# A new order of tasks for a pre-norm block of Infini attention and a dense MLP, on one core

## The chip, the core and the metric

The kernel runs on one core of a Trainium2 chip. A core has a matrix engine (TensorE, PE in the profile), a vector engine (VectorE, DVE), an activation engine (ScalarE, ACT), a general engine (GpSimd, POOL), and a queue from which this kernel issues all its transfers (SyncE, SP). They run side by side and wait for one another on semaphores. The metric is the device time of one execution in microseconds (us); smaller is better.

## The reference

A sequence of 2048 tokens with 640 features goes through one transformer block:

```python
h  = x + attention(layernorm(x))
h2 = h + silu(layernorm(h) @ w1) @ w2          # w1: 640 x 1728, w2: 1728 x 640
```

The attention has 32 heads of 20 features and goes through the sequence in 4 segments of 512 tokens. Each segment does causal softmax attention inside itself, and reads a memory that holds the segments before it:

```python
for s in range(4):
    p     = softmax(q_s @ k_s.T * scale + mask);  a_dot = p @ v_s
    pq    = phi(q_s)                               # phi(t) = t + 1 if t > 0 else exp(t)
    a_mem = (pq @ M) / (pq @ z + 1e-6)
    o_s   = g * a_mem + (1 - g) * a_dot            # g = sigmoid(beta), per head
    M += phi(k_s).T @ v_s;  z += phi(k_s).sum()
out = concat(o_s) @ wo
```

Inputs and output are in bf16.

## The kernel before

The kernel is a list of 1313 tasks with declared reads and writes. `build` declares them segment by segment, and `Graph.schedule` (L291 on) walks through the list `ORDER`, in which the tasks' numbers stand, and gives each its buffer slot and a planned start. What the program keeps of this is the order on each engine, the buffers, and the number of filler matmuls on a zero tile in the first microseconds. Each engine works strictly through its own list; `Tracker` puts in the semaphore waits that the data ask for. The string `ENGINE` says for each task which engine does it (p, a, d, g, s for PE, ACT, DVE, POOL, SP), and `BANK` which PSUM bank a result gets. So an instruction that waits holds up all that follow on its engine, and a transfer that cannot be issued yet holds up all transfers behind it.

The planned times come from costs in the source: for compute tasks a duration, for transfers a time on SP, a time `bw` on the shared transfer engines, and a time until landing. They are never seen by the chip.

The names of the tasks, with segment `s`, token block `b` (of 128 tokens) or chunk `c` (of four heads and some):

- `x{b}`, `w_k0`, `w_q0`, `w_wv`, `w_wo*`: loads of tokens and weights. `w_w1_0` to `w_w1_4` and `w_w2_0` to `w_w2_8` are the MLP's weights.
- `re_wq{j}`, `re_wk{j}`: pieces of the q and k weights copied into a layout with 32 columns a head (`wqr`, `wkr`, L798 and L799), on ScalarE, VectorE or GpSimd.
- `n1_st`, `n1_rs`, `n1_ap`, `n1_tr` (and `n2_...` before the MLP): statistics, reciprocal root, application and transpose of a layer norm for one block (L828, L868, L878, L916). The first four blocks are transposed by TensorE (`n1_tp`) and copied out (`n1_tc`, L900 and L901).
- `v{s}{i}` and `ve{s}{i}`: projection to v (L943) and its evacuation (L953 on ScalarE, L954 on VectorE). `pr{s}{c}{w}` and `qe{s}{c}{w}`: projection to q (`w`=0) or k (1) (L971) and its evacuation (L981, L982). `ex`, `ph`: the exponential and phi.
- `vt{s}{n}`: 16 small copies a segment (L1011) that bring spare rows of `QK` into the tile `QKV`, from which heads 20 to 31 are worked.
- `kt{s}{c}`, `mz{s}{c}`, `ma`, `mb`: transposed phi(K) (L1196), its product with V (L1204), adding it to the memory, and the masked copy of it.
- For each of 32 ticks `k` (8 groups of four heads in each segment): `qk{k}..` scores (L1052), `e{k}..` their exponentials (L1063), `mk` the causal mask (L1074), `av` the product with V (L1102), `oe` its evacuation (L1115, L1118), `tn` the product with the memory and the transposing product (L1134, L1138), `nm` and `ad` the division and the sum (L1153, L1165 to L1171, L1179).
- `ot{b}`, `wo{b}`, `rs{b}`: transpose of the attention's output (L1264), output projection (L1272), residual (L1280).
- `h1_{s}_{f}`, `th`, `s{s}_{f}`: first MLP product (L1300, L1295), tanh and silu (L1314, L1319; L1308 in the last segment). `h2_{b}_{q}`, `o{b}`, `out{b}`: second MLP product (L1360, L1335), residual (L1370), store.

The stages overlap: while segment s is in its ticks, the MLP of segment s-1 and the projections of segment s+1 fill TensorE.

Of the kernel before, what the change touches and what calls it, by code (L numbers as in the profile page):

```python
# [1430 lines left out]
```

## Time and profile before

| | |
|---|---|
| time of 3 runs | 309.59, 310.88, 311.26 us; median 310.88 us |
| the profiled execution | 312.17 us, of which the span from first to last instruction is 310.3 us |
| granted TensorE clock, mean | 0.994 |
| busy: PE, ACT, DVE, POOL | 291.9, 223.5, 214.1, 150.0 us |
| moved by DMA | 24.61 MB |

In the rows shown below, a group line gives the source line, the engine, the operation, the tiles and shapes and the count, then the busy time and the mean of one in ns, then the idle time just before and what ended it. A line of a window gives the stretch, its length, then the busy time and count of instructions for PE, its weight loads, DVE, ACT and POOL, then the granted clock of TensorE (1.00 is full), the busy share of the transfer engines and the GB/s they moved. A line of a timeline gives start and length, and in brackets the idle time before it with its releaser. A transfer line gives count, size of one and the median time from issue to landing.

### The profile page before, as it was taken

To read this page: it belongs to the slowest core of one execution; us is meant where nothing else is said; L and a number is where in the kernel's file an instruction comes from. 1 tells how busy PE (TensorE), PEld (TensorE's weight loads), DVE (VectorE), ACT (ScalarE), POOL (GpSimd) and SP (SyncE) were. 2 spreads that over 40 slices of the span, in tenths; PEclk is the share of its full clock that TensorE was granted. 3 is DMA by queue.
4 is the path that set the end of the run, shared out by engine and by line. 5 is a ranking of instruction groups with operands and counts; after the bars stand their busy time and mean duration, and the time that the engine had idled before them with its cause. 6 is when DMAs were issued, how large, how long until landed. Compare 5 with 4: busy or idle time off the path is not lost.

```text
span 310.3 us, 6823 instructions
## 1 busy us (share of the span) xinstructions
PE 291.9 (94%) x2674; PEld 159.4 (51%) x2702; DVE 214.1 (69%) x435; ACT 223.5 (72%) x291; POOL 150.0 (48%) x293
## 2 busy tenths in 40 slices
PE   8799897879989999999999999999999999999996
PEld 6454443435534444666555544464654457664574
DVE  4689988796887979864678768658997763940022
ACT  3599997988887998878887689877979972004400
POOL 2979947471463465556454436465684551210000
PEclk9999999988999999999999999999999999999999
DMA  7835519566473073533331200032430002340022
GB/s 215 288 89 113 88 29 222 130 142 117 85 140 60 15 231 69 83 66 67 77 41 28 58 2 2 15 55 49 97 66 0 3 3 42 86 101 26 2 95 74
DMA packets 51103, 24.61 MB, mean 79 GB/s; under 512 B 39680, under 2 KB 49792, under 8 KB 51072
## 3 DMA queue, kind: packets, MB, share of 16 engines
q1 hardware_dynamic: 51072, 24.19, 35.3%
q8 instruction: 21, 0.34, 0.5%
q14 instruction: 10, 0.08, 0.1%
HBM read 10.41 MB, written 2.62 MB: 42 GB/s over the span
## 4 chain that ended last, share of the span: by engine, by line
PE 67%; ACT 12%; DVE 9%; DMA 6%; issue 3%; SPq 1%; POOL 0%; POOLq 0%; ACTq 0%; DVEq 0%
PE ps_gen L1360 16%; PE ps_gen L971 10%; PE ps_gen L1300 9%; PE ps_sc L1052 6%; PE ps_gen L943 5%; PE ps_gen L1102 5%; PE ps_sc L1300 4%; PE ps_gen L1272 4%; ACT PTB L1063 4%; ACT PTA L1063 3%; ACT th L1314 2%; DMA nT<-xn_rot 2%; PE ps_gen L1134 2%; DVE stt L828 2%; PE ps_gen L1204 2%
## 5 line engine op out<-in xcount | busy, mean ns | idle before, releaser
L1063 ACT ACTIVATE PTA<-ps_sc 128x1024 bf16<-128x1024 f32 x64 | 62.4, 1021 | 11.2 <-PE ps_sc L1052 10.7
L1063 ACT ACTIVATE PTB<-ps_sc 128x1024 bf16<-128x1024 f32 x64 | 62.1, 1022 | 9.4 <-PE ps_sc L1052 9.2
L1074 POOL TENSOR_SCALAR_AFFINE_SELECT PTB<-PTB 128x512 bf16<-128x512 bf16 x64 | 41.7, 652 | 42.6 <-ACT PTB L1063 40.5
L1360 PE MATMUL ps_gen<-w_sb,sT 128*128 128x320 bf16 x420 | 61.4, 299 | 0.6 <-DVE x_tok L1280 0.6
L1360 PEld LDWEIGHTS ps_gen<-w_sb,sT 128*128 128x128 bf16 x420 | 39.4, 98 | 19.3 <-issue 2.2
L1300 PE MATMUL ps_gen<-nT,w_sb 128*128 128x512 bf16 x185 | 45.1, 380 | 1.3 <-DVE sT L1319 0.5
L1319 DVE SCALAR_TENSOR_TENSOR sT<-th,ps_gen 128x512 bf16<-128x512 f32 (+1 forms) x42 | 27.6, 664 | 13.2 <-ACT th L1314 12.7
L1063 ACT ACTIVATE PTE<-ps_sc 128x1024 bf16<-128x1024 f32 x32 | 31.1, 1025 | 2.9 <-PE ps_sc L1052 2.8
L828 DVE BATCH_NORM_STATS2 stt<-x_tok 128x6 f32<-128x320 bf16 x62 | 27.0, 477 | 3.8 <-DMA x_tok<-in_A_x_dram 3.5
L1074 POOL TENSOR_SCALAR_AFFINE_SELECT PTE<-PTE 128x512 bf16<-128x512 bf16 x32 | 20.7, 648 | 17.2 <-ACT PTE L1063 16.0
L1308 ACT ACTIVATE sT<-ps_sc 128x512 bf16<-128x512 f32 (+1 forms) x14 | 7.8, 581 | 28.4 <-PE ps_sc L1300 28.3
L1300 PEld LDWEIGHTS ps_gen<-nT,w_sb 128*128 128x128 bf16 x195 | 17.3, 98 | 20.8 <-issue 2.0
L1074 POOL TENSOR_SCALAR_AFFINE_SELECT PTA<-PTA 128x512 bf16<-128x512 bf16 x32 | 20.4, 640 | 15.4 <-ACT PTA L1063 15.3
L1314 ACT ACTIVATE th<-ps_gen 128x512 f32<-128x512 f32 (+1 forms) x42 | 24.3, 589 | 5.0 <-PE ps_gen L1300 4.3
L1179 POOL TENSOR_TENSOR otok<-on 128x320 bf16<-128x320 bf16 x24 | 19.3, 813 | 14.1 <-DVE on L1171 14.1
L982 DVE CAST QK<-ps_gen 128x512 bf16<-128x512 f32 x29 | 19.8, 684 | 7.9 <-PE ps_gen L971 7.9
L1272 PE MATMUL ps_gen<-wo_sb,oT 128*128 128x320 bf16 x160 | 23.8, 299 | 0.9 <-DMA oT<-otok 0.5
L971 PE MATMUL ps_gen<-nT,wkr 128*128 128x512 bf16 x93 | 23.2, 379 | 1.0 <-issue 0.8
L943 PE MATMUL ps_gen<-wv_sb,nT 128*128 128x320 bf16 x160 | 24.0, 299 | 0.0
L971 PE MATMUL ps_gen<-nT,wqr 128*128 128x512 bf16 x91 | 22.8, 379 | 1.1 <-issue 0.7
L1370 DVE SCALAR_TENSOR_TENSOR x_tok<-ps_gen,x_tok 128x640 bf16<-128x640 f32 x15 | 12.4, 824 | 16.1 <-PE ps_gen L1360 15.8
L1052 PE MATMUL ps_sc<-QK 20*128 20x256 bf16 (+3 forms) x320 | 20.4, 304 | 2.4 <-ACT PTA L1063 1.1
(104 smaller groups left out, 459.6 us busy)
## 6 DMA issues: line engine op xcount, KB each, us to landing
x_tok<-in_A_x_dram SPq DMA_DIRECT2D x16, 160.0 KB, 4.9
out_dram<-x_tok SPq DMA_DIRECT2D x15, 160.0 KB, 1.9
w_sb<-in_B_w_dram SPq DMA_DIRECT2D x5, 432.0 KB, 3.7
w_sb<-in_B_w_dram SPq DMA_DIRECT2D x6, 320.0 KB, 5.2
QKV<-QK SPq DMA_DIRECT2D x16, 72.0 KB
sT<-in_A_wk_dram SPq DMA_DIRECT2D x2, 400.0 KB, 5.2
sT<-in_A_wq_dram SPq DMA_DIRECT2D x2, 400.0 KB, 5.8
wv_sb<-in_A_wv_dram SPq DMA_DIRECT2D x1, 800.0 KB, 8.7
```

The lines of the kernel that those rows point to most:

```text
L828: T.add(DV, lambda e, hh=hh: e.bn_stats(out=stt[:, s, 6 * hh:6 * hh + 6], in_=xb[:, 320 * hh:320 * hh + 320]), reads=R((xa, xsub)), writes ...
L943: fns.append(lambda e, c=c, hh=hh: e.matmul(bank(ps, hh)[:, 0:320], lhsT=xT[:, c, 128 * i:128 * i + 128], rhs=wv_sb[:, c, :].rearrange("p ...
L971: fns = [lambda e, kc=kc: e.matmul(bank(ps), lhsT=wt[:, kc, c, :], rhs=xT[:, kc, :], start=(kc == 0), stop=(kc == NC - 1)) for kc in range ...
L982: (lambda e: e.tensor_copy(out=o, in_=bank(ps)))
L1052: fns.append(lambda e, j=j, o=o, n=n, r=r, qa=qa, ka=ka: e.matmul(sc_all[:, o:o + n], lhsT=ka[32 * r:32 * r + DH, 128 * j:128 * j + 128], ...
L1063: T.add(AC, lambda e: e.activation(out=pt[:, pta.slot, q0:q0 + 2, :], in_=sc3[:, b0:b0 + 2, :], func=ACT.Exp, scale=SCALE), reads=[("sc", ...
L1074: fns.append(lambda e, v=v: e.affine_select(out=v, in_=v, pattern=[[0, 4], [1, 128]], compare_op=ALU.is_ge, fill=0.0, base=0, channel_mult ...
L1272: fns.append(lambda e, c=c, hh=hh: e.matmul(bank(ps, hh)[:, 0:320], lhsT=oT[:, c, 128 * i:128 * i + 128], rhs=wo_sb[:, c, 320 * hh:320 * h ...
L1300: fns = [lambda e, c=c: e.matmul(bank(ps), lhsT=w1_sb[:, c, 128 * f:128 * f + 128], rhs=hT[:, c, :], start=(c == 0), stop=(c == NC - 1)) f ...
L1314: T.add(AC, lambda e: e.activation(out=th[:, tha.slot, 0:nt], in_=bank(ps)[:, 0:nt], func=ACT.Tanh, scale=0.5), reads=R((ps, [0])), writes ...
L1319: T.add(DV, lambda e: e.scalar_tensor_tensor(out=sT[:, f, 0:nt], in0=th[:, tha.slot, 0:nt], scalar=1.0, in1=bank(ps)[:, 0:nt], op0=ALU.add ...
L1360: fns.append(lambda e, f=f, hh=hh: e.matmul(bank(ps, hh)[:, 0:320], lhsT=s_of(i, f), rhs=w2_of(i, f, 320 * hh), start=(f == 0), stop=(f == ...
```

## The change

No instruction is added or taken away but for possibly another count of fillers. Three things change.

First, the planner's costs. Transposes take less of the transfer engines and land later, weight loads take more of them:

```diff
-        begun = False
...
-                if t.bw > 1.0 and not begun:
-                    begun = True
-                    dmaq += 1.45
                 free[e] = max(st + cost, dmaq - 8.0)
-                t.end = t.ready = dmaq + (1.25 if tr else 1.4)
+                t.end = t.ready = dmaq + (1.75 if tr else 1.4)
...
-        cost = {"tr": 1.27, "plain": 0.46, "bulk": 0.46, "sb": 0.71}[kind]
+        cost = {"tr": 1.28, "plain": 0.46, "bulk": 0.46, "sb": 0.85 if bw > 0.8 else 0.71}[kind]
...
-        load_x(b, 1, -200 + b, (0.5, 0.5, 0.9, 0.9)[b], "plain")
+        load_x(b, 1, -200 + b, (0.5, 0.5, 2.0, 0.46)[b], "plain")
...
-        load_w(f"w1_{c}", ..., wp[4] + 0.3 * c, 1.25, [(W["w1"], [c])])
+        load_w(f"w1_{c}", ..., wp[4] + 0.3 * c, 1.7, [(W["w1"], [c])])
...
-        load_w(f"w2_{k}", ..., wp[5] + 0.3 * k, 0.95 if k < 6 else 0.5,
+        load_w(f"w2_{k}", ..., wp[5] + 0.3 * k, 1.2 if k < 6 else 0.7,
...
-        G.task(f"mt{k}", {PO: 0.65}, e_mt, ...)
+        G.task(f"mt{k}", {PO: 0.93}, e_mt, ...)
...
-            prio, 1.3, "tr")
+            prio, 0.75, "tr")
...
-                    G.task(f"ph{s}{c}{w}", {DV: 0.95}, e_phi, ...)
+                    G.task(f"ph{s}{c}{w}", {DV: 1.04}, e_phi, ...)
...
-                G.task(f"ad{k}", {PO: 0.82}, e_ad, ...)
+                G.task(f"ad{k}", {PO: 0.78}, e_ad, ...)
...
-                                                                  in_=phiK[:, pka.slot, :]), pr, 1.15, "tr")
+                                                                  in_=phiK[:, pka.slot, :]), pr, 0.6, "tr")
```

(The transposes `ot` change like `n1_tr`, from 1.3 to 0.75.)

Second, the lists `ORDER`, `ENGINE` and `BANK` are new. In names, TensorE's first tasks were, and are now:

```
before  n1_tp0 n1_tp1 n1_tp3 n1_tp2 pr001 pr000 qk000 pr010 pr011 qk010 v02 v03 qk020 v01 pr020 qk100 pr021 v00 qk110
        pr031 av0 qk200 pr030 pr040 qk210 mz00 pr041 av1 qk220 mz01 v12 qk300 v10 qk310 v11 tn1 av2 qk400 pr121 pr101 tn0
        qk410 pr100 pr111 qk420 av3 tn2 pr110 qk500 mz02 pr140 mz03 qk510 pr130 av4 qk600 v13 mz04 qk610 pr131 mz10 qk620
        tn4 pr141 av5 qk700 tn3 mz11 pr120 qk710 av6 mz12 tn5 qk800 tn6 mz13 av7 v22 qk810 tn7 mz14 v23 qk820 v20 v21
        qk900 wo3 wo0 qk910 av8 wo1 qk1000 pr201 wo2 qk1010 pr211 pr200 qk1020 av9 tn8 pr220 qk1100 pr221 pr210 qk1110
        tn9 h1_0_2 ...
now     n1_tp0 n1_tp1 n1_tp2 n1_tp3 pr001 pr000 pr011 qk000 v03 qk010 pr010 v02 qk020 pr021 pr020 qk100 v01 v00 qk110
        pr031 av0 qk200 pr041 pr040 qk210 pr030 mz00 mz01 qk220 v12 av1 qk300 v10 tn0 tn1 qk310 pr100 av2 qk400 pr101 v11
        qk410 tn2 pr111 mz02 av3 qk420 pr121 pr140 qk500 pr110 mz03 qk510 av4 pr130 qk600 mz04 pr131 qk610 tn3 v13 qk620
        av5 pr141 mz10 qk700 tn4 mz11 pr120 qk710 tn5 av6 mz12 mz13 tn6 qk800 av7 v22 qk810 tn7 mz14 v23 qk820 v20 v21
        qk900 wo3 wo0 qk910 wo1 pr201 av8 qk1000 wo2 av9 qk1010 pr211 pr200 tn8 qk1020 pr221 pr220 qk1100 pr210 tn9
        h1_0_2 ...
```

The rest of TensorE's list is close to the old one. At its end, where `h2_12_0` stood inside the last `h1_3_*` and `h2_12_1 h2_12_2 h2_15_2 h2_15_3` behind them, it now has `h2_15_2 h2_15_3 h2_12_0 ...` behind them.

SP's queue of transfers:

```
before  x0 x1 x3 x2 w_k0 w_q0 w_k1 w_q1 x8 beta0 w_wv x6 x10 x4 x5 x11 beta1 x7 x9 kt00 w_wo4 w_wo0 w_wo7 kt01 n1_tr4
        n1_tr6 vt08 vt00 vt04 n1_tr5 vt012 n1_tr7 vt05 vt013 vt03 vt010 vt014 vt01 vt011 vt015 vt02 vt06 vt07 vt09 w_w1_0
        kt02 w_w1_3 kt03 w_w2_0 kt04 n1_tr8 w_w1_2 kt10 w_wo2 w_wo3 kt11 w_wo1 w_wo6 kt12 w_w1_1 n1_tr10 kt13 n1_tr11 x14
        kt14 n1_tr9 w_wo5 x12 vt18 ot3 ot0 vt112 vt10 ot1 vt14 vt115 ot2 vt16 w_w1_4 x15 vt19 n2_tr3 n2_tr0 n2_tr1 n2_tr2
        (9 more vt1*) w_w2_8 kt20 w_w2_5 w_w2_3 w_w2_2 w_w2_4 x13 w_w2_1 w_w2_7 kt21 w_w2_6 ...
now     x1 x3 x0 x2 w_k0 w_q0 w_k1 beta0 w_q1 w_wv x5 x6 x4 x7 x9 w_wo7 x10 beta1 kt00 n1_tr6 vt04 vt00 n1_tr4 w_wo2 kt01
        vt08 vt012 n1_tr7 n1_tr5 x11 vt014 vt05 vt01 vt02 vt07 x8 kt02 vt03 vt015 vt013 vt011 vt06 vt09 vt010 w_w1_2 kt03
        w_w1_0 kt04 w_wo5 kt10 w_wo0 w_w1_3 n1_tr8 n1_tr11 kt11 n1_tr10 w_wo3 kt12 kt13 w_wo4 vt112 vt10 vt16 kt14 n1_tr9
        w_wo1 w_wo6 vt14 ot3 ot0 ot1 ot2 vt18 x15 w_w1_1 vt111 w_w1_4 n2_tr3 vt110 n2_tr0 n2_tr1 n2_tr2 vt17 vt11 x14 vt19
        vt115 vt113 vt12 vt15 vt13 vt114 w_w2_1 x12 w_w2_2 x13 w_w2_0 w_w2_7 w_w2_4 w_w2_5 w_w2_6 w_w2_3 kt20 kt21 w_w2_8 ...
```

Third, 48 tasks change their engine: 22 go from DVE to ACT and 14 from ACT to DVE (evacuations for the most part), 12 pieces of the weights' new layout go to or from POOL. From DVE to ACT: `re_wk0 re_wk7 n1_tc3 ve01 qe001 qe020 ve11 qe130 oe9 oe14 oe15 ve20 ve23 qe210 qe230 qe240 qe241 oe20 ve33 qe320 qe331 qe341`. From ACT to DVE: `re_wk9 n1_tc2 qe021 qe041 oe6 qe120 oe8 oe11 oe17 ve31 ve32 qe330 oe25 oe31`. Of the pieces, `re_wk1 re_wk2 re_wq9` go from POOL to ACT and `re_wq5 re_wq8 re_wk3 re_wk5` from ACT to POOL. On VectorE, where `n2_ap1 qe200 n2_ap2` stood, there is now `n2_ap1 n2_ap2 qe200`.

More of the change, by code (lines that the diff above doesn't have):

```diff
@@ new lines @@
+    "sppppdsppppdsdgdsdgdsdgdsdgdspapapdpdpdadpaadpdadpdadpdadpdadpaadpdadpdadpdadssssssssssssssssspdgspd"
+    "gspdgspdgspdgpaagpaagpaagpdpdgpaagpaagpapdgpaagpaagpaagpapdgpaagpaagpdpdgpaagpaagpaagpapdgpaagpaagpd"
+    "pdgpaagpaagpaagpapdgpaagpaagpapdgspddgdsspddgdsspddgdsspddgdspadpadpadpadpadpadpadpadpadpadpadpadpad"
+    "padppppdsppppdsppppdsppppdsdgdsdgdsdgdsdgdspapapdpapdadpaadpaadpaadpdadpdadpaadpdadpaadpaadsssssssss"
+    "sssssssspdgspdgspdgspdgspdgpaagpaagpaagpdpdgpaagpaagpdpdgpaagpaagpaagpapdgpaagpaagpdpdgpaagpaagpaagp"
@@ L517 @@
+    "apdgpaagpaagpdpdgpaagpaagpaagpdpdgpaagpaagpdpdgspddgdsspddgdsspddgdsspddgdspadpadpadpadpadpadpadpadp"
+    "adpadpadpadpadpadppppdsppppdsppppdsppppdsdgdsdgdsdgdsdgdspapdpdpapaadpapdadpdpaadpapdadpapdadpasssss"
+    "ssssssssssspaagpaagpaagpdpdgpaagpaagpdpdgpaagpaagpaagpapdgpaagpaagpdpdgpaagpaagpaagpdpdgpaagpaagpdpd"
+    "gpaagpaagpaagpdpdgpaagpaagpdpdgspddgdsspddgdsspddgdsspddgdspapapapapapapapapapapapapapappppdsppppdsp"
     "pppdsppdsppds"
@@ L519 @@
 BANK = (
-    "0200022113320210200133110120332021100222010001003121033002202210213030021313310101222202203230202020"
-    "3332011223210020022221313022132223002202010303012200020213223001330300220002011100132012212302011102"
-    "210002220201"
+    "0202222110012201313113100100330332210200011302210320003002222202021320210121013021320211103220202020"
+    "3332013213030020022222032330122330321212011200011200020211323001030102020002001301033003212302012213"
+    "210002202023"
 )
@@ L683, in build @@
     for c in range(NC):
-        load_w(f"w1_{c}", w1_sb[:, c, :], B_w1[128 * c:128 * c + 128, :], wp[4] + 0.3 * c, 1.25, [(W["w1"], [c])])
+        load_w(f"w1_{c}", w1_sb[:, c, :], B_w1[128 * c:128 * c + 128, :], wp[4] + 0.3 * c, 1.7, [(W["w1"], [c])])
     for k in range(7):
         f0, f1 = 2 * k, min(2 * k + 2, NF - 1)
-        load_w(f"w2_{k}", w2_sb[:, f0:f1, :], cw(B_w2[128 * f0:128 * f1, :]), wp[5] + 0.3 * k, 0.95 if k < 6 else 0.5,
+        load_w(f"w2_{k}", w2_sb[:, f0:f1, :], cw(B_w2[128 * f0:128 * f1, :]), wp[5] + 0.3 * k, 1.2 if k < 6 else 0.7,
                [(W["w2"], [k])])
@@ L762, in e_mt @@
                 channel_multiplier=-1), reads=R((MT, [0])), writes=R((MT, [0])))
-        G.task(f"mt{k}", {PO: 0.65}, e_mt, [(C, ["beta_bc0"])], [(MT, [0])], 1)
+        G.task(f"mt{k}", {PO: 0.93}, e_mt, [(C, ["beta_bc0"])], [(MT, [0])], 1)
     blk_type = {0: 0, 2: 0, 4: 0, 6: 0, 9: 0, 1: 1, 3: 1, 5: 1, 7: 2, 10: 2, 8: 3, 11: 3}
@@ L1002, in declare_front @@
                     prp = k0 + pv("phq", s) + pv("phqc", s) * c if w == 0 else k0 + pv("phk", s) + pv("phkc", s) * c
-                    G.task(f"ph{s}{c}{w}", {DV: 0.95}, e_phi, [(qk[c], [w]), (exa, [0])], [(pa, ["a"])], prp)
+                    G.task(f"ph{s}{c}{w}", {DV: 1.04}, e_phi, [(qk[c], [w]), (exa, [0])], [(pa, ["a"])], prp)
         qv = G.alloc("QKV")
@@ L1182, in e_ad @@
                         reads=R((ona, [0])), writes=R(*osub))
-                G.task(f"ad{k}", {PO: 0.82}, e_ad, [(ona, [0])], osub, k + pv("nm", s))
+                G.task(f"ad{k}", {PO: 0.78}, e_ad, [(ona, [0])], osub, k + pv("nm", s))
         sg["ota"] = ot
@@ L1264, in declare_back @@
                 lambda e, i=i: e.dma_start_transpose(out=oT[:, :, 128 * i:128 * i + 128], in_=otok[:, i, :]),
[L1265 removed]
+                pr, 0.75, "tr")
             ps = G.alloc("ps", 2, False)
```

16 lines of the change are left out of this document (3 added, 13 removed), and 120 rows, old and new, of the table ORDER.

## The prediction, made before the changed kernel was run

> **What bounds the kernel now.** I read the head of the page first, then the busy time by stage, then TensorE's own timeline where a stage is not full. The head:
>
> ```profile
> span 310.3 us, 6823 instructions
> ...
> PE 291.9 (94%) x2674; PEld 159.4 (51%) x2702; DVE 214.1 (69%) x435; ACT 223.5 (72%) x291; POOL 150.0 (48%) x293
> ...
> PE 67%; ACT 12%; DVE 9%; DMA 6%; issue 3%; SPq 1%; POOL 0%; POOLq 0%; ACTq 0%; DVEq 0%
> ```
>
> TensorE is busy 291.9 of 310.3 us, and it holds 67% of the chain that ended last. Its work is not changed, so the most that an order can win is the 18.4 us in which it stands, and what it loses to a lower clock. By stage (span, then busy us of PE, weight loads, DVE, ACT, POOL; granted clock; DMA share; GB/s):
>
> ```profile
> 0.00:12.00 12.00, 9.74 (x67) 7.02 (x69) 6.39 (x17) 5.48 (x10) 6.12 (x23) 1.00 0.74 225
> 12.00:44.00 32.00, 29.95 (x262) 15.05 (x267) 27.36 (x63) 28.65 (x41) 26.73 (x70) 1.00 0.45 111
> 44.00:60.00 16.00, 13.74 (x134) 6.39 (x136) 13.25 (x31) 14.11 (x18) 7.89 (x16) 1.00 0.81 172
> 60.00:80.00 20.00, 17.49 (x186) 9.61 (x187) 15.29 (x34) 17.13 (x23) 9.72 (x17) 0.91 0.57 115
> 80.00:100.00 20.00, 18.15 (x164) 8.88 (x164) 16.30 (x33) 16.52 (x20) 9.94 (x20) 1.00 0.56 100
> 100.00:260.00 160.00, 156.50 (x1568) 83.69 (x1585) 120.95 (x233) 133.79 (x170) 86.55 (x141) 1.00 0.25 50
> 260.00:280.00 20.00, 18.73 (x130) 12.40 (x129) 11.07 (x23) 0.80 (x2) 3.04 (x8) 1.00 0.44 99
> 308.00:310.30 2.30, 0.00 (x0) 0.00 (x0) 0.15 (x1) 0.00 (x0) 0.00 (x0) 1.00 0.12 36
> ```
>
> From 12 to 100 us TensorE stands 2.05 + 2.26 + 2.51 + 1.85 = 8.67 us of 88, and 60 to 80 us is the one stage with a clock below 1. From 100 to 260 us it stands only 3.5 us of 160. The first 12 us (start-up) and the last 2.3 us (the last output's way out) have no other matmul to give. So the stage to read is 12 to 100 us, and this is also where the new order differs most: of TensorE's 355 tasks, 124 of the first 206 have another place, 35 of the rest.
>
> **The change part by part.** The refitted costs are not in the program; they act only through the order and engines found with them, and through the slots that the planner gives by its times. I cost those at nothing themselves.
>
> The waits of TensorE that I can name in this stage (start, length, instruction, in brackets the idle time before it and its releaser):
>
> ```profile
> 14.64 0.39 PE L1052 MATMUL ps_sc<-QK 20*128 20x512 bf16 x4 [0.69 <-ACT QK L981]
> ...
> 52.62 0.66 PE L1204 MATMUL ps_gen<-Vx,phiKt 128*128 128x288 bf16 x4 [1.36 <-DMA phiKt<-phiK]
> ...
> 66.70 0.40 PE L1102 MATMUL ps_gen<-PTA,Vx 128*32 128x512 bf16 x4 [0.75 <-DVE Mz L1233]
> ...
> 68.17 0.77 PE L1204 MATMUL ps_gen<-Vx,phiKt 128*128 128x192 bf16 x4 [0.74 <-DVE otok L1153]
> ...
> 92.99 0.34 PE L1134 MATMUL ps_gen<-Mzb,phiQ 128*128 128x96 bf16 x4 [1.16 <-DVE QK L982]
> ```
>
> *Start-up.* The first projection starts here, and `w_w1_1` and the last `w_w2` load go out, and the second matrix of the MLP is first used, at these times:
>
> ```profile
> 11.84 1.03 PE L971 MATMUL ps_gen<-nT,wkr 128*128 128x512 bf16 x4
> ...
> 62.91 0.58 SPq L651 DMA_DIRECT2D w_sb<-in_B_w_dram  x1
> ...
> 114.72 0.57 SPq L651 DMA_DIRECT2D w_sb<-in_B_w_dram  x1
> ...
> 124.96 2.33 PE L1360 MATMUL ps_gen<-w_sb,sT 128*128 128x320 bf16 x16
> ```
>
> Of the token blocks, `x1 x3 x0 x2` are loaded in place of `x0 x1 x3 x2`; block 2 stays last, and its statistics set the start. ScalarE now makes the first two pieces of `wkr` (`re_wk0`, `re_wk1`) ahead of its copies `n1_tc1`, `n1_tc0`. The load of that half takes 5.2 us from its issue by the row below; it comes fifth as before, so the pieces can start near 8 us, when ScalarE has nothing else. If it is late, the copies wait behind them. I take 0, with 0 to +0.5 us.
>
> *First scores (`qk000`).* They waited 0.69 us for ScalarE's evacuation of `pr000`. In the new order a projection, `pr011`, stands ahead of them. But `qe001` goes from VectorE to ScalarE, so the first exponentials start a little later. I take -0.4, between -0.69 and +0.3.
>
> *The transposed phi(K) of chunk 3 (`kt03`, `mz03`).* Two weight loads stood beside it:
>
> ```profile
> 47.44 5.13 DMA phiKt<-phiK
> ...
> 87.50 4.29 DMA nT<-xn_rot
> ```
> ```profile
> w_sb<-in_B_w_dram SPq DMA_DIRECT2D x5, 432.0 KB, 3.7
> w_sb<-in_B_w_dram SPq DMA_DIRECT2D x6, 320.0 KB, 5.2
> sT<-in_A_wk_dram SPq DMA_DIRECT2D x2, 400.0 KB, 5.2
> nT<-xn_rot SPq DMA_TRANSPOSE x28, 2.7
> phiKt<-phiK SPq DMA_TRANSPOSE x15, 2.6
> ```
>
> Half of these transposes land within 2.6 us; this one took 5.13 and cost TensorE 1.36 us. The new queue has all `w_w2` loads behind the copies `vt1*`, and `kt02` ahead of seven of the copies `vt0*`; one `w_w1` load still stands directly ahead of `kt03`. The 2.5 us that the transpose can lose cover the 1.36. I take -1.0, between -1.36 and 0.
>
> *The thin stretch from 64.7 to 68.1 us.* The same view in stretches of 3.4 us, for the three thinnest places and for the one after the first:
>
> ```profile
> 50.00:53.40 3.40, 2.04 (x20) 0.83 (x17) 2.46 (x7) 2.30 (x3) 3.18 (x7) 1.00 1.24 235
> 64.70:68.10 3.40, 1.74 (x27) 0.55 (x25) 3.33 (x8) 3.30 (x5) 2.00 (x4) 1.00 0.75 197
> 68.10:71.50 3.40, 3.33 (x24) 1.88 (x28) 2.17 (x6) 2.65 (x4) 2.10 (x3) 0.52 0.59 134
> 91.00:94.40 3.40, 2.19 (x36) 1.08 (x29) 2.06 (x4) 2.51 (x4) 2.86 (x5) 1.00 0.50 103
> ```
>
> TensorE was busy 1.74 of 3.40 us (51%), and the clock of the next 3.4 us fell to 0.52: 3.40 x 0.48 = 1.6 us of matmul time lost. Stretches with 60% (2.04) and 64% (2.19) were followed by no such fall. So a little more work in this one saves its idle time and the whole 1.6 us. VectorE was full there (3.33 of 3.40), and the two waits inside, 0.75 and 0.74 us, are for VectorE. The new order puts `tn5` ahead of `av6` and `mz13` directly behind `mz12`, so more matmuls that need no fresh VectorE result stand here. But of the evacuations near it, `qe130` leaves VectorE and `oe6` and `qe120` come, one more than before; what helps is that `ve01`, `qe001`, `qe020` and `ve11` left it earlier. I take -0.4 for the waits (0 to -1.49) and -1.6 for the clock (0 to -1.6; it is one or the other, and 0.3 us more work in the stretch brings it to the 60% that kept its clock).
>
> The Trainium skill ("TensorE: Matmul & The Clock Gate", section "HAM oscillation — how this bites in real kernels") puts its rule as "no PE-idle gaps >~3.4µs". Here the clock fell with no gap in the 3.4 us before it longer than the 0.75 us above, so the measurement goes against reading the rule as the only condition. By that rule a denser order wins no clock, and the sum would lack this term.
>
> *`tn8`.* Its 1.16 us stand at the end of a chain: the transpose of 87.50 us (4.29) holds up an application of the second norm on VectorE, behind it waits the evacuation of a projection, and behind that `tn8`. The new order moves `av9` and `tn8` ahead of `qk1020`, but on VectorE it puts `n2_ap1` and `n2_ap2` both ahead of `qe200`, so the same wait would still reach it. I take 0, between -1.16 and +1.16.
>
> *SP's queue.* It is nearly full while the copies `vt0*` go out:
>
> ```profile
> 27.44 2.52 SPq L916 DMA_TRANSPOSE nT<-xn_rot  x2
> ...
> 36.58 8.45 SPq L1011 DMA_DIRECT2D QKV<-QK  x12
> ...
> 45.56 1.20 SPq L1196 DMA_TRANSPOSE phiKt<-phiK  x1
> ...
> 85.77 0.44 SPq L651 DMA_DIRECT2D w_sb<-in_B_w_dram  x1
> ```
>
> From 27.44 to 45.03 us it issues four transposes and 16 copies, the last 12 at 0.70 us each. In the new queue `kt01`, `kt02`, `x11`, `x8` and a piece of `wo` stand among them: 2 x 1.20 + 3 x about 0.45 = 3.8 us more between the first and the last. `kt01`, `x11`, `x8` and most of `wo` only change sides, and by my estimate the first of the group can go out some 2 us earlier, since `n1_ap6` and `pr020` each move up by more than one task. All 16 must land before `qk420`, which the new order puts behind `tn2`, `mz02` and `av3`, with `pr121` moved away: about 0.4 us later. If that cover is gone, TensorE waits there. I take +0.5, between 0 and +2.
>
> *ScalarE's share.* Evacuations up to 100 us: four of `ve`, four of `qe` and one of `oe` come over from VectorE, three of `qe` and two of `oe` go back.
>
> ```profile
> L1115 ACT ACTIVATE oTs<-ps_gen,lsc 128x512 bf16<-128x512 f32 x11 | 7.6, 690 | 2.2 <-PE ps_gen L1102 2.1
> L981 ACT ACTIVATE QK<-ps_gen 128x512 bf16<-128x512 f32 x11 | 6.6, 602 | 2.1 <-PE ps_gen L971 2.0
> L953 ACT ACTIVATE Vx<-ps_gen 128x640 bf16<-128x640 f32 x6 | 4.2, 705 | 2.5 <-PE ps_gen L943 2.5
> ```
>
> 4 x 0.705 + 1 x 0.602 - 1 x 0.690 = +2.7 us; the weight pieces that ScalarE gains hold fewer elements than those it loses (1,280 against 1,920 per partition), so +2.2 us or so. In the 88 us it stands 11.6 us, which cover it; uncovered it costs 2.2. ScalarE's part of the chain is 12%: 12% of 2.2 is +0.3, between 0 and +2.2.
>
> *The MLP's loads.* `w_w1_1` (issued at 63 us before) and `w_w1_4` now both stand just ahead of the transposes `n2_tr0` to `n2_tr3`, where one did. `h1_0_2` needs all four transposes. One more 432 KB load is worth at most its 3.7 us; the projections `pr201` to `pr210`, which stand ahead of `h1_0_2`, cover most of it. I take +0.3, between 0 and +3.7. The last `w_w2` load went out 10.2 us (124.96 - 114.72) before its first use, against 5.2 us to land; eight of the nine now go out ahead of `kt20` and the ninth directly behind `kt21`, as the last did before, so 0.
>
> *After 100 us* the order is nearly the old one. The end changes by putting `h2_15_2` and `h2_15_3` directly behind the last `h1_3_*`; the seven matmuls of the first stand between the last activation and its use: 0. Bounds for all this are -1 and +1, a third of the 3.5 us to either side.
>
> Sum: -0.4 - 1.0 - 0.4 - 1.6 + 0 + 0.5 + 0.3 + 0.3 = -2.3 us. The profiled execution took 312.17 us (span 310.3 and 1.87 around it), so 309.9 by its own time. It lies 1.29 us above the median of the runs, 310.88, so on that scale the forecast is 308.6 us.
>
> **The rivals.**
>
> *The half-speed stretch stays or turns up elsewhere.* For it: 51% stands near 60%, and every reordering makes thin places of its own; 50 to 53.4 and 91 to 94.4 us were close. Against it: the waits inside it are the ones that move. Without the -1.6 the time is 310.2. This is also what the rule above, of the Trainium skill's page "TensorE: Matmul & The Clock Gate", gives.
>
> *The waits go almost all.* All named ones at their full size: -0.69 - 1.36 - 1.49 - 1.6 - 1.16 = -6.3, with nothing given back: 304.6. Against it: all engines are above 80% busy from 12 to 44 us, POOL too.
>
> *The new order stalls elsewhere as much as it saves.* For it: the old order stands 8.7 us in this stage without one long stall, in many short ones, and a new order meets the same loads and the same full engines. 310.9, within 0.5%, which is about what a measurement of this kernel can tell from no change.
>
> *Slower: the first hidden layer starts late.* Two 432 KB loads ahead of `n2_tr0` to `n2_tr3` push them back by up to 3.7 us; the old ones took 4.29 us from 87.50 already and were on the chain. If TensorE runs out of `pr2*` before they land, it stands up to 3.7 us near 97 us, falls under half busy over 3.4 us, and loses 1.6 us of clock. In place of the +0.3 this gives -2.6 + 5.3 = +2.7, or 313.6. It decides only if the whole load is uncovered; TensorE keeps at least 60% of a 3.4 us stretch as long as the wait stays under 1.4 us, and then the clock need not fall and the case ends near 310.
>
> **How the numbers follow.** The forecast 0.37, half-speed stretch kept 0.15, almost all waits gone 0.12, evenly given back 0.18, slower 0.18. The forecast's own range is 306.9 to 310.2. The range reaches from the case of 304.6 to just short of the slow one's middle: 304.6 to 313.2. Faster by over 0.5% means under 309.33: some three quarters of the forecast's case, the case of 304.6, and a quarter of the second and fourth together, 0.48. Slower means over 312.43: nearly all of the slow case, 0.17. Between them 0.35.
>
> **What would show it.** Right: no clock below 0.95 in any 3.4 us between 60 and 75 us; TensorE idle under 7 us between 12 and 100 us; the matmuls of line 1204 without a DMA wait over 0.5 us; line 1052's first without a wait on `QK`; line 1134 with its wait on a line 982 evacuation, about as now. Wrong: line 1052 waiting over 1 us for `QKV` near 47 us; line 1300's first matmuls waiting on `nT` near 97 us; ScalarE over 95% in any 20 us of the stage with line 1052 waiting on line 1063 more than now; a clock of 0.5 in a new place; a start of the first projections of line 971 after 12.4 us.

## The result, and the profile after

The changed kernel took 307.49 us in the median of four runs (306.28 to 308.05), the kernel before 311.07 us beside it (309.59 to 314.23). The ratio is 0.9871 [0.9826, 0.9915]: faster by 1.3%, and 1.1 us faster than the forecast of 308.6. The profiled execution of after took 306.28 us. It is the fastest of its four, while that of before (312.17 us) is slower than the three runs given with it, so the two profiles differ by more (5.8 us of span) than the medians do (3.6 us). All lines of the kernel after stand four lower than before (the scores of line 1052 are now at 1048, phi(K) times V of line 1204 at 1200, the first MLP product of 1300 at 1296).

The head of the page after:

```profile
span 304.5 us, 6832 instructions
...
PE 289.3 (95%) x2678; PEld 159.3 (52%) x2708; DVE 208.8 (69%) x428; ACT 225.3 (74%) x298; POOL 150.0 (49%) x293
...
PE 70%; ACT 12%; DVE 6%; DMA 5%; issue 3%; SPq 2%; POOL 1%; POOLq 0%; ACTq 0%; DVEq 0%
```

The same stages as in the prediction, and the place of the old thin stretch:

```profile
0.00:12.00 12.00, 10.04 (x77) 7.50 (x79) 6.29 (x17) 6.29 (x11) 7.24 (x26) 1.00 0.73 214
12.00:44.00 32.00, 29.89 (x269) 15.04 (x271) 27.28 (x65) 29.38 (x41) 22.78 (x59) 1.00 0.50 117
44.00:60.00 16.00, 14.39 (x148) 6.72 (x150) 13.90 (x31) 15.73 (x20) 12.05 (x28) 1.00 0.79 171
60.00:80.00 20.00, 18.74 (x194) 11.02 (x194) 15.24 (x35) 18.62 (x24) 11.17 (x19) 1.00 0.49 98
80.00:100.00 20.00, 19.73 (x175) 8.82 (x178) 16.46 (x35) 18.37 (x25) 11.19 (x20) 1.00 0.57 137
100.00:260.00 160.00, 155.96 (x1563) 85.53 (x1578) 117.19 (x225) 129.39 (x167) 82.44 (x134) 1.00 0.26 50
...
64.70:68.10 3.40, 2.71 (x46) 1.53 (x35) 3.30 (x9) 3.40 (x6) 2.38 (x5) 1.00 0.43 77
```

From 12 to 100 us TensorE stands 2.11 + 1.61 + 1.26 + 0.27 = 5.25 us, where it stood 8.67. The old thin stretch is 80% busy (2.71 of 3.40), and the clock is 1.00 throughout. From 12 to 44 us nothing was won. From 100 to 260 us the idle time reads 4.0 us against 3.5, but a second profile of the changed kernel (after_again, below) reads 1.9 there, so no loss is shown. The gain lies between 44 and 100 us.

TensorE's own timeline shows which waits these were. The rows that answer to the waits quoted before, in order of time:

```profile
15.01 1.26 PE L939 MATMUL ps_gen<-wv_sb,nT 128*128 128x320 bf16 x8 [0.47 <-DMA wv_sb<-in_A_wv_dram]
...
45.82 0.29 PE L1048 MATMUL ps_sc<-QK 20*128 20x256 bf16 x4
...
49.83 0.65 PE L1200 MATMUL ps_gen<-Vx,phiKt 128*128 128x288 bf16 x4
...
67.18 0.40 PE L1098 MATMUL ps_gen<-PTA,Vx 128*32 128x512 bf16 x4 [0.69 <-POOL PTB L1070]
...
86.60 0.33 PE L1130 MATMUL ps_gen<-Mzb,phiQ 128*128 128x96 bf16 x4
...
91.60 1.03 PE L1296 MATMUL ps_gen<-nT,w_sb 128*128 128x512 bf16 x4
```

`mz03` at 49.83, `tn8` at 86.60 and the first hidden layer at 91.60 have no wait in brackets. Two waits are new: 0.47 us for the load of `wv` at the start, and 0.69 us for GpSimd's mask at 67.18, in place of the two VectorE waits of 0.75 and 0.74 us.

The second profile, after_again, also has no wait at `mz03`, `tn8` and the first hidden layer, and it stands 5.80 us from 12 to 100 us. But two waits are in it that the first profile does not have, one of them at the first scores:

```profile
15.51 0.39 PE L1048 MATMUL ps_sc<-QK 20*128 20x512 bf16 x4 [0.99 <-ACT QK L977]
...
71.98 0.67 PE L1200 MATMUL ps_gen<-Vx,phiKt 128*128 128x96 bf16 x8 [0.64 <-DMA phiKt<-phiK]
```

SP's own timeline, which the prediction had read as nearly full:

```profile
21.00 1.20 SPq L912 DMA_TRANSPOSE nT<-xn_rot  x1
22.78 1.84 SPq L1007 DMA_DIRECT2D QKV<-QK  x2
...
36.93 1.22 SPq L1192 DMA_TRANSPOSE phiKt<-phiK  x1
38.20 4.92 SPq L1007 DMA_DIRECT2D QKV<-QK  x7
...
43.66 1.21 SPq L1192 DMA_TRANSPOSE phiKt<-phiK  x1
```

The first of the group of transposes and copies goes out at 21.00 (27.44 before). `kt02` at 36.93 stands among the copies, the last of which are out at 43.12 (45.03 before). `kt03` follows at 43.66 (47.44 before). The transfers issued from 43 to 45 us, with count, size and time from issue to landing:

```profile
phiKt<-phiK SPq DMA_TRANSPOSE x1, 5.3
```

So `kt03` takes 5.3 us to land, as it took 5.13 before. It lands in time because it is issued 3.8 us earlier. In the second profile the group starts at 22.37, the last copies are out at 44.48 and `kt03` follows at 45.01.

### The profile page after: what moved, and what is told of

Same layout as the page of the kernel before. It is cut to its first block, busy times and chain, and to the rows that moved or that the text cites. A ratio compares the mean times of both kernels' runs of the same rounds, so it can differ in the third digit from the quotient of the medians.

```text
span 304.5 us, 6832 instructions
## 1 busy us (share of the span) xinstructions
PE 289.3 (95%) x2678; PEld 159.3 (52%) x2708; DVE 208.8 (69%) x428; ACT 225.3 (74%) x298; POOL 150.0 (49%) x293
## 4 chain that ended last, share of the span: by engine, by line
PE 70%; ACT 12%; DVE 6%; DMA 5%; issue 3%; SPq 2%; POOL 1%; POOLq 0%; ACTq 0%; DVEq 0%
PE ps_gen L1356 15%; PE ps_gen L1296 11%; PE ps_gen L967 10%; PE ps_sc L1048 7%; PE ps_gen L939 6%; PE ps_gen L1268 5%; PE ps_gen L1098 5%; PE ps_sc L1296 5%; ACT PTA L1059 4%; ACT PTB L1059 3%; DMA wv_sb<-in_A_wv_dram 3%; PE ps_gen L1130 2%; DMA nT<-xn_rot 2%; ACT PTE L1059 2%; DVE stt L824 2%
## 5 line engine op out<-in xcount | busy, mean ns | idle before, releaser
L1059 ACT ACTIVATE PTA<-ps_sc 128x1024 bf16<-128x1024 f32 x64 | 62.2, 1023 | 7.9 <-PE ps_sc L1048 6.2
L967 PE MATMUL ps_gen<-nT,wqr 128*128 128x512 bf16 x95 | 24.0, 380 | 1.0 <-ACT Vx L949 0.5
L967 PE MATMUL ps_gen<-nT,wkr 128*128 128x512 bf16 x87 | 22.4, 380 | 1.2 <-issue 0.6
L1167 DVE TENSOR_TENSOR on<-ps_gen,rd 128x640 bf16<-128x640 f32 x24 | 19.8, 824 | 0.8
```

Source lines behind the costliest of these rows:

```text
L967: fns = [lambda e, kc=kc: e.matmul(bank(ps), lhsT=wt[:, kc, c, :], rhs=xT[:, kc, :], start=(kc == 0), stop=(kc == NC - 1)) for kc in range ...
L1059: T.add(AC, lambda e: e.activation(out=pt[:, pta.slot, q0:q0 + 2, :], in_=sc3[:, b0:b0 + 2, :], func=ACT.Exp, scale=SCALE), reads=[("sc", ...
L1167: T.add(DV, lambda e: e.tensor_tensor(out=on[:, ona.slot, :, :].rearrange("p b (x e) -> p b x e", e=DH), in0=v[:, :, :, 0:DH], in1=r2.unsq ...
```

## The experiments

All were timed in five rounds against the kernel before. Three questions stood open: which of order, engines and banks carries the gain; which stretch of the kernel does; and whether single waits, taken away one by one in the old kernel, bring it.

### Engines alone, order alone

```diff
 engines_only:  old ORDER and BANK
-ENGINE = old
+ENGINE = new
 order_only:  old ENGINE
-ORDER, BANK, costs = old
+ORDER, BANK, costs = new
```

> The old order, banks and costs, but the 48 tasks on their new engines. Theory: the order carries the gain, since each engine's list decides what waits; moving evacuations alone takes VectorE work out of the full stretch from 64 to 68 us but puts it on ScalarE: ratio 0.995 to 1.006. Rival (VectorE's load is what was relieved, 5.3 us less of it in the profile): ratio 0.985 to 0.991, with the clock at 1.00 from 60 to 80 us.

> The new order, banks and costs, but all tasks on their old engines. Theory: keeps more than half of the gain, ratio 0.986 to 0.994, losing most at the start, where the two first pieces of wkr go back to VectorE and GpSimd (first projection of line 967 at 11.5 to 11.9 us in place of 11.0). Rival (VectorE's load): ratio above 0.996.

Measured: engines alone 328.39 us (325.20 to 330.65), ratio 1.0555 [1.0495, 1.0616]; order alone 322.55 us (321.62 to 323.25), ratio 1.0386 [1.0337, 1.0434]. Each half is slower than either whole. Both theories fall, and so does the rival of the first; the second's rival (VectorE's load) allowed a ratio above 0.996, but does not explain a loss of 3.9%. The first projection with the order alone starts at 12.12, later still than the 11.5 to 11.9 expected. The waits of TensorE in the kernel with the engines alone (total, times, longest, in us):

```profile
PE ps_sc L978 <- ACT PTA L989: 5.4, 8, 1.7
PE ps_sc L978 <- ACT PTB L989: 3.3, 6, 1.8
PE ps_gen L1060 <- ACT oTs L1041: 2.7, 1, 2.7
```

And with the order alone:

```profile
PE ps_gen L1060 <- ACT QK L903: 2.5, 1, 2.5
PE ps_sc L974 <- ACT PTA L985: 2.3, 4, 1.1
PE ps_gen L865 <- DVE Mz L1155: 1.5, 1, 1.5
```

With the engines alone, evacuations that ScalarE took over stand in its list at places that were chosen for VectorE, and the exponentials (`PTA`, `PTB`) come late behind them. With the order alone it is the evacuation of a projection that ScalarE does late. This is read from the waits; no run took them away. A place in a strictly ordered list and the engine that the list belongs to cannot be judged one without the other, so nothing follows for either one's own worth.

### The old order up to the MLP, or the new one

In these hybrids a prefix (order, engines and banks together) comes from one kernel and the rest of the order, engines and banks from the other. All hybrids of this section and the next carry the new costs.

```diff
 new_to_mlp:  the 507 tasks that the old ORDER has ahead of h1_0_2
-in old order, engines, banks
+in new order, engines, banks          (the rest old)
 old_to_mlp:  all but the 507 tasks that the new ORDER has ahead of h1_0_2
-in old order, engines, banks
+in new order, engines, banks          (the 507 old)
```

The two sets of 507 differ in six tasks, so the second hybrid is not the exact complement of the first, as its expectation has it. Its old beginning lacks the loads `w_w2_0` and `x12`, which come later, and has five more of the copies `vt1*`.

> The 507 tasks that the old order has ahead of the first MLP matmul (h1_0_2, 97.8 us before, 91.6 us in the new kernel) stand in the new order, on the new engines and banks; all later tasks stand as in the old kernel. Theory: the gain is the shortened waits ahead of 98 us, worth 6.2 us in the profiled execution, some 1.6 us of it the clock. Then this kernel gains about what the whole change gains: ratio 0.985 to 0.991 to the kernel before, h1_0_2 starting at 91 to 92.5 us. Rival (the gain is spread over the kernel, through fewer VectorE evacuations in all four segments): under half, ratio above 0.993.

> The complement: the 507 tasks up to the first MLP matmul stand in the old order on the old engines, all later ones as in the new kernel. Theory: nothing gained after 98 us: ratio 0.997 to 1.003, h1_0_2 at 97 to 98.5 us. Rival (gain spread over the kernel): ratio below 0.994.

Measured: the new beginning 308.61 us (307.55 to 309.52), ratio 0.9941 [0.9911, 0.9971]; the new end 309.40 us (307.88 to 311.54), ratio 0.9971 [0.9941, 1.0001]. The beginning carries a measurable part; for the end no gain is shown. In the second, `h1_0_2` starts at 94.95 and not at 97 to 98.5. The first has two waits at its seam (TensorE's timeline):

```profile
93.32 0.40 PE L974 MATMUL ps_sc<-QK 20*128 20x384 bf16 x8 [0.79 <-ACT PTA L985]
94.11 2.10 PE L1222 MATMUL ps_gen<-nT,w_sb 128*128 128x512 bf16 x9 [0.39 <-ACT QK L903]
```

Its `h1_0_2` starts at 94.11 and not at 91.60. So the next hybrids were cut where the new order has the cut.

### How much of the beginning is needed

```diff
 after_again:    the kernel after, unchanged
 prefix_mlp:     the new list up to h1_0_2 (507 tasks), the rest as before
 prefix_v22:     the new list up to v22    (395 tasks, some 68 us), the rest as before
 prefix_qk600:   the new list up to qk600  (300 tasks, some 53 us), the rest as before
```

> The changed kernel once more, with more runs, beside the partial ones. Theory: the first comparison's ratio of 0.987 took in executions of the old kernel with a half-speed stretch of TensorE (10 of 23 runs of the old kernel had a mean clock of 0.994 or 0.995); the change's ratio lies at 0.988 to 0.992, with no run under a clock of 0.999. Rival: it is 0.984 to 0.988.

> Everything that the new order has ahead of the first MLP matmul (507 tasks) exactly as in the new kernel, the rest in the old order. (new_to_mlp had cut along the old order instead; at its seam one transpose and one score stood in the way of TensorE, 0.6 and 0.8 us.) Theory: the gain lies ahead of the seam: h1_0_2 starts at 91.5 to 92.5 us as in the new kernel, ratio within 0.003 of after_again. Rival (the rest of the order carries some of it, as old_to_mlp's 0.997 may say): ratio 0.004 or more above after_again, with h1_0_2 at 91.5 to 92.5 us all the same.

> The new order up to the projection v22 (395 tasks, some 68 us), the rest in the old order. Theory: the thin stretch from 64 to 68 us is filled, so no run shows a clock under 0.999, and v22 starts at 67.5 to 69 us: ratio 0.990 to 0.995. Rival (the gain comes from 68 to 98 us, through the evacuations ve20 and ve23 on ScalarE and the loads of x and of w_w2): ratio above 0.996.

> The new order only up to the scores qk600 (300 tasks, some 56 us), the rest in the old order. Theory: the start (0.5 to 0.8 us) and the shorter waits up to mz03 (some 1 us) stay, the stretch from 60 to 98 us is as before: ratio 0.994 to 0.998. Rival (the start alone carries what is gained): same ratio as prefix_v22 and after_again.

| kernel | median us (range) | ratio to before, with interval |
|---|---|---|
| after_again | 307.50 (306.97 to 310.22) | 0.9902 [0.9867, 0.9938] |
| prefix_mlp | 308.55 (307.65 to 311.76) | 0.9920 [0.9895, 0.9945] |
| prefix_v22 | 310.08 (308.63 to 312.25) | 0.9990 [0.9957, 1.0022] |
| prefix_qk600 | 307.32 (306.94 to 307.89) | 0.9884 [0.9858, 0.9911] |

The last matmuls of prefix_qk600's new list end at 53.3 us on TensorE. These first 53 us of the new list are enough: with the old list behind them, the kernel cannot be told from the whole change.

Both expectations for the shorter prefixes missed, that of prefix_qk600 on the good side. It had taken the stretch from 60 to 98 us to stay as before. But there too the waits shrank: the one of 0.75 us for VectorE is 0.21, TensorE is busy 2.22 of the 3.40 us from 62.2 on, and none of the six runs has a clock under 1.000. In prefix_v22 three of 12 runs have 0.994 or 0.995. Its ratio is the one its rival named, but since prefix_qk600 gains all with the old list from 53 us on, the rival's cause, the new order from 68 to 98 us, is not needed. The ratios of after_again and prefix_mlp came out as expected, but one of six and one of 12 of their runs have a clock of 0.994 (310.22 and 311.76 us), where no run of after_again was to lie under 0.999; which stretch lost it no trace shows. And prefix_mlp starts `h1_0_2` at 94.71, behind a wait of 0.79 us at 94.13 as in new_to_mlp. So it is not shown that the place of the cut set that hybrid back, and their intervals overlap.

The middle prefix shows that it is no matter of more being better. Its seam makes stalls of its own, here in TensorE's timeline:

```profile
71.33 0.33 PE L1060 MATMUL ps_gen<-sel,oTs 128*128 128x96 bf16 x4 [0.80 <-DVE Mz L1155]
...
78.50 2.89 PE L1194 MATMUL ps_gen<-wo_sb,oT 128*128 128x320 bf16 x20 [1.50 <-DMA oT<-otok]
```

Compare prefix_qk600 with x_order (below), whose execution also kept its clock at 1.000 and which has the old list but for the first loads. Counted from each one's first projection, so that the start-up drops out (us):

| milestone | x_order | prefix_qk600 | lead |
|---|---|---|---|
| first scores on `QKV` | 35.73 | 35.23 | 0.50 |
| `mz03` | 41.05 | 39.14 | 1.91 |
| `tn8` | 80.10 | 76.39 | 3.71 |
| first hidden layer, `h1_0_2` | 84.90 | 81.19 | 3.71 |
| end of the last matmul | 294.82 | 291.34 | 3.48 |

Three steps make the lead, and each has a wait of x_order's TensorE ahead of it:

```profile
46.41 0.29 PE L978 MATMUL ps_sc<-QK 20*128 20x256 bf16 x4 [0.73 <-DMA QKV<-QK]
...
51.84 0.66 PE L1130 MATMUL ps_gen<-Vx,phiKt 128*128 128x288 bf16 x4 [1.07 <-DMA phiKt<-phiK]
...
90.89 0.34 PE L1060 MATMUL ps_gen<-Mzb,phiQ 128*128 128x96 bf16 x4 [1.49 <-DVE QK L908]
```

The same instructions in prefix_qk600:

```profile
46.02 0.29 PE L974 MATMUL ps_sc<-QK 20*128 20x256 bf16 x4
...
50.04 0.65 PE L1126 MATMUL ps_gen<-Vx,phiKt 128*128 128x288 bf16 x4
...
87.29 0.34 PE L1056 MATMUL ps_gen<-Mzb,phiQ 128*128 128x96 bf16 x4
```

The three waits add up to 0.73 + 1.07 + 1.49 = 3.29 us. The lead grows by 0.50, 1.41 and 1.80 us at the three places, so the waits account for most of it, though not one for one. These are one execution of each kernel. The third wait goes although the list around it is the old one, so it hangs on what came earlier. Other profiles agree: the six whose beginning is new in order and engines (after, after_again, new_to_mlp and the three prefixes) have no such wait, and before, x_order, x_order_kt02 and av6_twice have it with 0.79 to 1.49 us. The new beginning is not the only thing that takes it away: old_to_mlp and loads_away have the old beginning with `w_w2_0` loaded later, and no such wait either. In x_order the second norm's transposes take SP from 85.08 us on, 1.26 us after the application that feeds the first of them starts on VectorE (83.82); in prefix_qk600 0.60 us after it (82.48 and 81.88). VectorE then stands 1.55 us ahead of a later application of the norm, and 0.45 us in prefix_qk600. The chain of x_order goes from such a transpose over the evacuation queued on VectorE to `tn8`:

```profile
86.35 3.44 DMA nT<-xn_rot
...
90.16 0.69 DVE QK L908
...
90.89 0.34 PE ps_gen L1060 x4
```

That SP comes late to these transposes because of its copies is my reading; no run took it away by itself.

### Single edits in the old kernel

```diff
 x_order
-x0 x1 x3 x2 ... n1_st0 n1_st3
+x1 x3 x0 x2 ... n1_st3 n1_st0
 x_order_kt02: as x_order, and
-(12 copies vt0*) w_w1_0 kt02 w_w1_3 kt03
+(5 copies) kt02 (7 copies) w_w1_0 kt03 w_w1_3
 loads_away
-w_w1_0 kt02 w_w1_3 kt03 w_w2_0 kt04
+kt02 kt03 kt04 w_w1_0 w_w1_3 w_w2_0
```

> The old kernel with one edit at the start: token blocks loaded as x1 x3 x0 x2 in place of x0 x1 x3 x2, and on VectorE the statistics of block 3 ahead of those of block 0. Theory: VectorE's gap between its first and second statistics (1.23 and 1.49 us in two profiles of the old start) closes, and the first projection (line 971 of the old kernel) starts at 10.9 to 11.3 us in place of 11.6 to 11.8; ratio 0.996 to 0.999. Rival (the new start gains by making the first pieces of wkr on ScalarE): first projection at 11.5 us or later, ratio 0.999 to 1.002.

> x_order, and in SP's queue the transpose kt02 moved up ahead of seven of the copies vt0*, and the load w_w1_3 moved from before kt03 to behind it, as the new queue has them. Theory: kt03 goes out some 1.8 us earlier and still takes about 5 us to land, but lands before TensorE wants it: mz03 (the first 128x288 matmul of line 1204) starts 2.0 to 2.6 us earlier than in the old profile; ratio 0.991 to 0.996, most of the whole change with five moved tasks. Rival (mz03 came early in the new kernel because other projections stand ahead of it on TensorE): the wait of about 1.4 us stays at least by half, ratio as x_order.

> The old kernel with the loads w_w1_0, w_w1_3 and w_w2_0 moved behind kt04, so that no weight load is in flight beside kt02 and kt03. This is the mechanism that the prediction gave for kt03. If it holds: kt03 lands in 2.3 to 3.0 us and the wait of mz03 is gone, ratio 0.994 to 0.998. Rival (transposes that follow each other, or the copies before them, make the landing long): kt03 takes over 4 us as before.

Measured: x_order 310.23 us (309.26 to 311.93), ratio 0.9990 [0.9958, 1.0022]; x_order_kt02 310.60 us (309.23 to 313.12), ratio 1.0020 [0.9992, 1.0049]; loads_away 309.41 us (307.68 to 312.53), ratio 0.9971 [0.9937, 1.0005]. None brings a gain that can be told from no change. The ratio of loads_away lies where its theory had it, but its interval takes in 1.

The order of the first loads shows no worth. The 11.84 us to the first projection in the profile of before were that execution's: profiled executions with the old loads and the old engines start it between 10.84 and 11.84, those with the new ones between 10.70 and 11.33.

x_order_kt02 is the most telling miss. `kt03` is on time (TensorE has no wait for it), but `mz03` starts at 53.04, no earlier than the 52.62 of before. `kt02` among the copies pushes the last of them back by its own 1.2 us, and TensorE waits for them, 0.9 us more than the 0.73 of x_order:

```profile
47.37 0.29 PE L978 MATMUL ps_sc<-QK 20*128 20x256 bf16 x4 [1.64 <-DMA QKV<-QK]
```

Its stretches of 3.4 us around this wait and around the two VectorE waits:

```profile
45.40:48.80 3.40, 1.71 (x31) 0.81 (x31) 1.85 (x5) 1.62 (x4) 1.45 (x3) 1.00 0.73 183
48.80:52.20 3.40, 3.40 (x14) 1.31 (x14) 2.82 (x7) 2.58 (x5) 2.23 (x5) 0.53 0.71 219
65.80:69.20 3.40, 1.75 (x36) 1.03 (x36) 3.30 (x9) 3.28 (x6) 2.07 (x4) 1.00 0.68 142
69.20:72.60 3.40, 3.40 (x31) 1.52 (x31) 2.30 (x7) 2.58 (x4) 2.10 (x3) 0.54 0.55 130
```

Twice TensorE is half busy (1.71 and 1.75 of 3.40), and twice the clock falls to half in the next stretch. This execution, with a mean clock of 0.989, is the only one of the 12 with more than one fall. This is what the prediction feared of the new queue ("If that cover is gone, TensorE waits there"). The new list starts the transposes and copies 5.1 to 6.4 us earlier in its two profiles, and that needs the earlier tasks in another order too. That this earlier start is what lets it escape is my reading; no run had the one without the other.

loads_away tests the prediction's mechanism for `kt03`. The three transposes, issued from 44.80 on with no load beside them (count, time to landing):

```profile
phiKt<-phiK SPq DMA_TRANSPOSE x3, 2.4
```

2.3 to 2.4 us each, against 3.6, 5.13 and 3.9 for the same three of before: the loads do hold the transposes up, and TensorE's wait for `kt03` is gone. But the loads then stand ahead of the next ones, and the wait comes back larger, 10 us later (TensorE's timeline, then the windows):

```profile
60.56 0.50 PE L1130 MATMUL ps_gen<-Vx,phiKt 128*128 128x192 bf16 x4 [2.45 <-DMA phiKt<-phiK]
```
```profile
58.70:62.10 3.40, 1.54 (x18) 0.88 (x19) 0.99 (x3) 1.37 (x3) 2.44 (x5) 0.87 0.86 240
62.10:65.50 3.40, 3.40 (x31) 1.23 (x29) 1.42 (x3) 1.90 (x4) 1.97 (x3) 0.62 0.80 135
```

The first of these stretches already holds the start of the fall (0.87). The 3.40 us just ahead of the fall, from 57.85 to 61.25, are 0.95 us busy. In 7 of the 12 runs of loads_away the clock is lowered.

### A fuller thin stretch

```diff
 av6_twice, in e_av
+                if s == 0 and g == 6:
+                    fns = fns + fns
```

The 16 matmuls of `av6` are issued twice, the second time over the first in the same bank; nothing else changes.

> The old kernel with one task's matmuls done twice into the same bank (av6, 16 matmuls, 0.66 us), in the 0.74 us in which TensorE waits behind it. The results stay the same; TensorE's busy time in the thin 3.4 us goes from 1.74 to 2.4 us. Theory (the clock falls when about half of such a stretch is idle): no run under a clock of 0.999, where 21 of 46 runs of the old kernel were; the median falls by 0.3 to 0.6 us, ratio 0.997 to 1.000. Rival (the fall does not hang on this stretch's busy share): about half of the runs at 0.994 again, ratio 1.000 to 1.003.

Measured: 309.80 us (308.59 to 310.76), ratio 0.9978 [0.9958, 0.9998]. The run's mean granted clock, in all 12 runs, was 0.999 or 1.000. The kernel before, over its 80 runs beside the experiments, had a mean clock of 0.995 or less in 40; their median is 311.34 us, that of the other 40 is 310.33. So a fall costs about 1.0 us, happens in half of that kernel's executions, and is worth some 0.5 us to a median. (If the nine longest of the 40 are left out, all over 1.5% above the fastest, their median is 311.16 and the cost 0.8 us. In the three groups alone it reads 0.7, 0.3 and 1.5 us, and the median of before lies 0.2, 0.3 and 0.7 us above the median of its executions at full clock.) With the stretch filled the falls are gone (none in 12 runs, against 19 in the 34 of before in that group), and the time is that of a full-clock execution of before: 309.80 in both cases in that group. The edit also cuts the wait behind `av6` from 0.74 to 0.20 us, so a fuller stretch and a shorter gap are not told apart. The stretch in av6_twice, and the same one in x_order:

```profile
64.00:67.40 3.40, 2.22 (x44) 0.91 (x43) 3.33 (x8) 3.28 (x5) 1.98 (x5) 1.00 0.62 148
```
```profile
64.00:67.40 3.40, 1.68 (x28) 0.54 (x27) 3.33 (x8) 3.28 (x5) 1.98 (x5) 1.00 0.49 110
```

x_order's is no fuller than that of before (1.68 against 1.74), and its execution kept the clock all the same.

## Why the prediction was right, point by point

Direction and range were right, and the time came out 1.1 us below the forecast, inside the forecast case's own range. The sum of -2.3 us stands against -3.6 in the medians. But the terms did not each come out: one was far too large, one had the wrong sign, one was left at nothing. That the sum came so near is in part luck, since the clock was put some 1.1 us too high and the 1.2 to 1.5 us of `tn8` were left out. The measured sizes are readings of single profiles; their middles add up to about -3.0 us, which is also what the ratio of after_again gives (0.9902).

| term | predicted | measured | from |
|---|---|---|---|
| start-up | 0 | 0 | starts overlap, see x_order |
| first scores | -0.4 | 0 to +1.2 | wait of 0.69 gone and 0.47 for `wv` in its place; 0.99 and 0.50 in the second profile |
| `kt03`, `mz03` | -1.0 | -1.1 to -1.4 | waits of 1.36 and 1.07 gone |
| thin stretch, waits | -0.4 | -0.8 | 0.75 + 0.74 against 0.69 |
| thin stretch, clock | -1.6 | about -0.5 | half of 1.0 us |
| `tn8` | 0 | -1.2 to -1.5 | waits of 1.16 and 1.49 gone |
| SP's queue | +0.5 | -0.3 to -0.7 | waits of 0.31 and 0.73 gone |
| ScalarE | +0.3 | +0.7 to +0.9 | scores' waits on `PTA` and `PTB`, 12 to 100 us: 1.7 to 2.1; a new wait of 0.3 to 0.5 for the evacuation of a `v` |
| MLP's loads | +0.3 | 0 | no wait ahead of `h1_0_2` |
| after 100 us | 0 | not shown | idle time 3.5 before, 4.0 and 1.9 in two profiles of after |

*First scores.* The first product with V (`av0`) starts 15.80 us after the first projection in the profile of before, and 15.69 and 16.96 in the two of after. Where the one wait went, its time moved to the next; in the second profile it did not go at all, and is longer than before.

*`kt03`.* Right in size, wrong in its step. "The 2.5 us that the transpose can lose" were not lost: it still lands in 5.3 us. What brings it in time is its earlier issue. The prediction had one of the moves behind that in hand (`kt02` ahead of seven copies) and used it only for the cost in SP's queue. By itself that move brings `kt03` out 0.9 us earlier (46.02 in x_order_kt02, 46.94 in x_order); the rest of the 3.8 us comes with the earlier start of the group.

*SP's queue.* The step that failed is the estimate that the group starts "some 2 us earlier": it starts 6.4 us earlier (21.00 against 27.44; 22.37 in the second profile), so the five added items of 3.8 us fit in, and the copies end 1.9 us earlier than before (0.5 us in the second profile). I had counted what was added to the stretch and not worked out when its first item becomes ready. With the old start the move of `kt02` raises this wait from 0.73 to 1.64 us (x_order, x_order_kt02); so the step's mechanism was right and its start wrong.

*Clock.* Mis-sized. A loss that the profile shows in full (1.6 us in that execution) was put in full into the median. The direct test says that it happens in half of the executions. The changed kernel is not quite free of it either: one of its ten runs has a clock of 0.994. Between 60 and 75 us the clock of after is 1.00, as the prediction said it would be. The Trainium skill ("TensorE: Matmul & The Clock Gate", section "What's actually happening") says that the activity window of about 3.4 us runs free and does not start with the kernel. That would make such a stretch a toss, and it agrees with 1.74 of 3.40 us having lost the clock here and 1.68 having kept it. The reading of its other rule, of no idle gap over 3.4 us, as the only condition is refuted further: the clock fell behind longest gaps of 0.75, 1.64 and 2.45 us.

*`tn8`.* Left at 0 because the order on VectorE just ahead of it looked the same. That its wait would stay "about as now" was wrong: with the old list there and the new one up to 34 us earlier (prefix_qk600) the wait is gone. It is also no constant of the old order: it is 0.79 us in av6_twice, 1.16 in before and 1.49 in x_order, and it is missing in old_to_mlp and loads_away.

*The rivals.* The half-speed stretch did not stay. The first hidden layer is not late (91.60, and 93.56 in the second profile, against 97.79, and no wait), so the slower case lost its place. What came true lies between the forecast and the case in which the waits go almost all.

*The signs.* Of those named for right, the clock and the idle time (5.25 us) came out, the wait of `tn8` did not stay, and two hold in the first profile and not in the second (the first scores' wait on `QK`, 0.99 us, and a wait of line 1200 for a transpose, 0.64 us). Of those named for wrong, one came: from 44 to 64 us ScalarE is busy 19.62 of 20 us, and the scores wait for the exponentials longer than before. Its price was small.

What stays open: the worth of the new costs by themselves (not tried), which of the 300 tasks' new places are needed for the earlier start of SP's group, and how much of the gain that start alone carries.

## What to carry to other kernels

When a transfer is late, read first when it was issued and what the queue did before that; how long it takes to land is the second question. A wait removed in one place of an in-order schedule can come back at a later item, as it did in two of the single edits here, so test a queue edit with the stretch behind it. A loss of clock that one profile shows should be weighed with the share of executions that have it, which the mean granted clock of every run tells. And half a change can cost more than the whole gains: here the new engines with the old order +5.6%, the new order with the old engines +3.9%, both together -1.3%.
